# Attention's transposes as 64-row array tiles, its scores in one four-bank tile, and eight blocks per evacuation

## The chip, the cores and the metric

The kernel runs on one core of a Trainium2 chip. The core has TensorE (PE in the rows; PEld is its weight load), VectorE (DVE), ScalarE (ACT), GpSimd (POOL) and SyncE (SP), each with its own queue of instructions that it works off in order; they wait for each other through semaphores. The metric is the device time of one execution in microseconds, as the median of several runs.

## The reference

Attention with a learned relative bias, and behind it two layers of experts. Attention has 2 batches, 8 heads, 576 positions and head size 64; everything is float32.

```python
scores = scale * np.matmul(q, k.transpose(0, 1, 3, 2))
psi_rel = np.log1p(np.abs(rel)); psi_i = np.log1p(np.maximum(pos[:, None], 1.0))
h = np.maximum((psi_rel / psi_i)[..., None] @ w1 + b1, 0.0)      # 32 hidden units
scores = scores + (h @ w2).transpose(2, 0, 1)[None, :, :, :]
attn = np.exp(scores - np.max(scores, axis=-1, keepdims=True))
attn = attn / (np.sum(attn, axis=-1, keepdims=True) + 1e-09)
x = np.matmul(attn, v)                        # then as 1152 rows of 512
out = sum(p[:, e:e+1] * (np.maximum(x @ w1[e], 0) @ w2[e]) for e in range(4))
# second layer: 8 experts, gates by 8 rounds of row and column normalisation
```

## The kernel before

Attention is cut into 36 units, numbered k = 0 to 35: 128 rows of the scores of one pair of heads (p) of one batch (b), by row tile t; in units 8 to 11 (t = 4) the 64 left-over rows of both batches share a unit. One loop over k writes the instructions of four units in different steps, and each engine executes them in the order written. With `u` for the unit a step belongs to, loop step k does this:

- `emit_x(k - 4)`: VectorE multiplies the finished output by one over the sums.
- `emit_S(k)`: TensorE makes the scores (12 matmuls; head 0 on array rows 0 to 63, head 1 on rows 64 to 127) into two PSUM tiles `sc`, one for each head, of two banks each. Behind them in the same tile come two transposes of unit k - 2, its "tail": the last 128 columns of the probabilities (64 per head), and `spread`, one over the sums copied out to 128 columns. Once the bias groups are done the tail goes to a tile `tl` and is written by `emit_T`.
- `emit_max(k)`: VectorE adds the bias and takes the row minimum of the negated scores, one instruction per head (L399).
- `emit_recip2(k - 1)`: VectorE's reciprocal, then GpSimd's copy to `spread`.
- `emit_exp(k, 0)` and `emit_exp(k, 1)`: ScalarE's exponentials, one per head (L412).
- `emit_T(k - 2)`: eight transposes of 128 x 128 (L444) into `tp0` and `tp1`, one bank each; `emit_evac` copies them to SBUF (`at`): four blocks (0), the tail (2), and after the second exponential the other four (1), by ScalarE while there are bias groups and by VectorE after that.
- `groups(1)`: one bias group, while there are any (`made < NGR`): TensorE's `bps` (L331), two ScalarE copies to `bsts` that empty it (L360), a store to DRAM. `bps` is one buffer. `hids` on VectorE makes the next group's operands.
- `emit_P(k - 3)`: probabilities times values (`po`, L470).

Bias groups last until k = 24. Beside attention the loop prepares the experts: `pieces` splits the input for layer 1 into two parts (L103 and L104; k = 16 to 18 and from 23), and from k = 28 the first expert weights are split, a high part by ScalarE (L169) and a low part by GpSimd (L170). At k = 36 the experts' first products start between the last steps of attention, and the tiles of the products take over the banks of the scores.

Of the kernel before, what the change touches and what calls it, by code (L numbers as in the profile page):

```python
# [9 lines left out]
F32 = mybir.dt.float32  # L10
# [38 lines left out]
def attn_moe_moe(ctx: ExitStack, tc: tile.TileContext, pack, keep, rel, qT, kT, vT, w, out):  # L49
# [134 lines left out]
    def attention(moe):  # L184
# [137 lines left out]
        def emit_bias_mm(g):  # L322
            _, _, n, nb = ranges(g)
            if nb == 1 and (made >= FIRST or made % 3 == 1):
                o = pt.tile([128, 1, 512], F32, tag="bps", name=f"bps{g}", bufs=1)
            else:
                o = ps.tile([128, 2, 512], F32, tag="sc", name=f"bps{g}", bufs=2)
# [42 lines left out]

        def emit_S(u):
            t, p, b = units[u]
            o = [ps.tile([128, 2, 512], F32, tag="sc", name=f"sc{u}{h}", bufs=2) for h in range(2)]

            todo = [(b, 0, 128, x, y) for x, y in ((0, 1), (1, 0), (0, 0))] if t < 4 else [(0, 0, 64, None, None), (1, 64, 64, None, None)]
            for j in range(2):
                for i, (bb, c, n, x, y) in enumerate(todo):
                    for h in range(2):
                        d = slice(64 * h, 64 * h + 64)
                        a, m = (qq[t, p][:, x], kk[p, bb][:, y]) if t < 4 else (rawq[t, p], rawk[p, bb])  # L380
                        pe.matmul(  # L381
                            out=o[h][c:c + n, j, 0:288],
                            lhsT=a[d, 128 * bb + c:128 * bb + c + n],
                            rhs=m[d, 288 * j:288 * j + 288],
                            start=t == 4 or i == 0,
                            stop=t == 4 or i == len(todo) - 1,
                        )
            for h in range(2):
                scps[u, h] = o[h]
            if 2 <= u and made < NGR:  # L390
                emit_tail(u - 2, sm[u - 2], o[1][:, :, 288:416])

        def emit_max(u):
            t, p, b = units[u]
# [31 lines left out]
            )  # L426

        tps = {}

        def emit_tail(u, s, o):  # L430

            pe.transpose(o[:, 1, :], s[:, 512:640], ident)  # L432
            pe.transpose(o[:, 0, :], spread.pop(u), ident)
            tps[u, 2] = o

        def emit_T(u):
            s = sm.pop(u)
            if (u, 2) not in tps:
                o = pt.tile([128, 1, 512], F32, tag="bps", name=f"tl{u}", bufs=1)
                emit_tail(u, s, o[:, 0, 0:256].rearrange("p (a c) -> p a c", a=2))  # L440
            for h in range(2):
                o = pt.tile([128, 4, 128], F32, tag=f"tp{h}", name=f"tp{u}{h}", bufs=1)
                for j in range(4):
                    pe.transpose(o[:, j, :], s[:, 640 * h + 128 * j:640 * h + 128 * j + 128], ident)  # L444
                tps[u, h] = o
        def emit_evac(u, h, eng):
            o = tps.pop((u, h))
            shape = [128, 4 if h < 2 else 2, 128]
            a = atb.tile(shape, F32, tag=f"at{h}", name=f"at{u}{h}", bufs=2)
# [4 lines left out]
            at_t[u, h] = a  # L454

        def emit_P(u):
            t, p, b = units[u]
            if b == 0:
                po[t, p] = po_all[:, tps_.index((t, p)) % 2, :]
            o = po[t, p]  # L460
            a = [at_t.pop((u, h)) for h in range(3)]
            rc[u] = a[2][:, 0, :]
            for bb in [b] if t < 4 else [0, 1]:
                n = 128 if t < 4 else 64
                c0, i0 = (128 * bb, 0) if t < 4 else (64 * bb, 64 * bb)
                for j in range(5):
                    for h in range(2):
                        col = (2 * bb + h) * D
                        rhs = a[h][:, j, i0:i0 + n] if j < 4 else a[2][:, 1, i0:i0 + n]
# [40 lines left out]
        order = list(range(8)) + list(range(32, NGR)) + list(range(8, 32))  # L510
        made = 0
        started = 0

        def hids(k, engs=()):
            nonlocal started
# [49 lines left out]
        ti, work, first_split = 0, [], None  # L565
        for k in range(U + 3):
            first = False
            if k < U:
                t, p, b = units[k]
                first = b == 0  # L570
# [15 lines left out]
            elif k == U:  # L586
# [453 lines left out]
```

## Time and profile before

| | us |
|---|---|
| median of 3 runs | 1346.22 (1346.18 to 1347.33) |
| profiled execution, whole | 1347.24 |
| its span in the profile | 1345.5 |
| TensorE busy, whole span | 1332.1 (99%) |
| VectorE, ScalarE, GpSimd busy | 780.0, 518.8, 433.3 |
| scores of unit 4 start | 47.66 |
| scores of unit 25 start (first unit without a bias group) | 138.93 |
| first expert product starts | 177.38 |

The profile is one execution. Busy time of TensorE is modelled, since its matmuls overlap; distances between starts say more. The chain of waits follows the work that ended last back from the end: where it stays on one engine, that engine was never kept waiting there.

### The profile page before, as it was taken

To read this page: it belongs to the slowest core of one execution; us is meant where nothing else is said; L and a number is where in the kernel's file an instruction comes from. 1 tells how busy PE (TensorE), PEld (TensorE's weight loads), DVE (VectorE), ACT (ScalarE), POOL (GpSimd) and SP (SyncE) were. 2 spreads that over 40 slices of the span, in tenths; PEclk is the share of its full clock that TensorE was granted. 3 is DMA by queue.
4 is the path that set the end of the run, shared out by engine and by line. 5 is a ranking of instruction groups with operands and counts; after the bars stand their busy time and mean duration, and the time that the engine had idled before them with its cause. 6 is when DMAs were issued, how large, how long until landed. Compare 5 with 4: busy or idle time off the path is not lost.

```text
span 1345.5 us, 22481 instructions
## 1 busy us (share of the span) xinstructions
PE 1332.1 (99%) x8783; PEld 1163.9 (87%) x8783; DVE 780.0 (58%) x1771; ACT 518.8 (39%) x1230; POOL 433.3 (32%) x455
## 2 busy tenths in 40 slices
PE   7999999999999999999999999999999999999998
PEld 4776888898898898898888988998988988988987
DVE  8788977463563553765764554644635635645533
ACT  6888863341331422443342421422422413313311
POOL 4533433260440530361440530621612603504400
PEclk9999999999999999999999999999999999999999
DMA  7875411130120110020120110210210201201010
GB/s 230 229 200 144 145 64 63 32 95 1 37 90 1 63 64 1 32 71 25 58 68 1 63 63 1 85 41 1 94 32 32 92 4 32 95 0 63 32 40 32
DMA packets 34313, 84.67 MB, mean 63 GB/s; under 512 B 8864, under 2 KB 9120, under 8 KB 34208
## 3 DMA queue, kind: packets, MB, share of 16 engines
q1 hardware_dynamic: 31184, 75.60, 18.0%
q0 software_dynamic: 2880, 7.34, 2.0%
q8 instruction: 69, 1.13, 0.3%
q10 hardware_dynamic: 144, 0.29, 0.1%
q14 instruction: 36, 0.29, 0.1%
HBM read 69.97 MB, written 13.25 MB: 62 GB/s over the span
## 4 chain that ended last, share of the span: by engine, by line
PE 94%; DVE 3%; ACT 1%; DMA 1%; issue 0%; SPq 0%; DVEq 0%; ACTq 0%
PE y L779 44%; PE B L700 17%; PE A L700 11%; PE C L700 11%; PE po L470 3%; PE sc L381 2%; PE tp L444 2%; PE bps L331 1%; ACT bsts L360 1%; DVE rows L801 0%; PE sc L432 0%; PE turn L868 0%; DVE wt L166 0%; DMA bt<-bd 0%; DVE hids L317 0%
## 5 line engine op out<-in xcount | busy, mean ns | idle before, releaser
L779 PE MATMUL y<-gb,h 128*128 128x512 f32 x2592 | 714.2, 396 | 0.0
L779 PEld LDWEIGHTS y<-gb,h 128*128 128x128 f32 x2592 | 451.0, 188 | 55.6
L170 POOL TENSOR_TENSOR gb<-rawb,gb 128x512 fp32r<-128x512 f32 x94 | 122.7, 1322 | 626.6 <-ACT gb L169 620.0
L708 DVE TENSOR_TENSOR u<-B,s 128x320 f32<-128x320 f32 (+1 forms) x192 | 87.9, 458 | 335.7 <-PE B L700 335.7
L711 ACT ACTIVATE h<-c 128x320 fp32r<-128x320 f32 (+1 forms) x288 | 119.8, 439 | 369.4 <-DVE c L708 367.9
L714 DVE SCALAR_TENSOR_TENSOR h<-c,h 128x320 fp32r<-128x320 f32 (+1 forms) x288 | 177.2, 632 | 51.0 <-ACT h L711 46.1
L170 POOL TENSOR_TENSOR ga<-rawa,ga 128x512 fp32r<-128x512 f32 x94 | 128.1, 1382 | 3.2 <-ACT ga L169 3.2
L170 POOL TENSOR_TENSOR ga<-wt,ga 128x512 fp32r<-128x512 f32 x94 | 106.6, 1153 | 25.4 <-ACT ga L169 12.4
L708 DVE TENSOR_TENSOR c<-C,u 128x320 f32<-128x320 f32 (+1 forms) x192 | 87.2, 454 | 38.4 <-PE C L700 34.6
L722 ACT ACTIVATE s<-A 128x320 f32<-128x320 f32 (+1 forms) x96 | 39.4, 411 | 166.5 <-PE A L700 166.3
L169 ACT ACTIVATE gb<-rawb 128x512 fp32r<-128x512 f32 x96 | 60.0, 626 | 85.2 <-DMA rawb<-in_w 85.2
L711 ACT ACTIVATE h<-A 128x320 fp32r<-128x320 f32 (+1 forms) x96 | 38.9, 405 | 136.5 <-PE A L700 136.3
L708 DVE TENSOR_TENSOR c<-B,s 128x320 f32<-128x320 f32 (+1 forms) x96 | 43.9, 457 | 76.3 <-PE B L700 75.3
L700 PE MATMUL C<-x20S,ga 128*128 128x320 f32 x384 | 66.7, 309 | 0.0
L700 PE MATMUL B<-x20S,ga 128*128 128x320 f32 x384 | 66.6, 309 | 0.0
L700 PE MATMUL A<-x20A,ga 128*128 128x320 f32 x384 | 66.6, 309 | 0.0
L700 PEld LDWEIGHTS A<-x20A,ga 128*128 128x128 f32 x384 | 61.5, 188 | 5.7
L700 PEld LDWEIGHTS C<-x20S,ga 128*128 128x128 f32 x384 | 61.3, 188 | 5.6
L700 PEld LDWEIGHTS B<-x20S,ga 128*128 128x128 f32 x384 | 61.3, 188 | 5.6
L412 ACT ACTIVATE s<-s,stat 128x576 f32<-128x576 f32 x72 | 55.7, 774 | 19.8 <-DVE stat L399 19.5
L700 PEld LDWEIGHTS C<-x21S,ga 128*128 128x128 f32 x384 | 54.4, 188 | 6.3 <-DVE c L708 0.7
L700 PEld LDWEIGHTS A<-x21A,ga 128*128 128x128 f32 x384 | 54.6, 189 | 5.6
(183 smaller groups left out, 1913.8 us busy)
## 6 DMA issues: line engine op xcount, KB each, us to landing
rawa<-in_w SPq DMA_DIRECT2D x48, 512.0 KB, 4.0
rawb<-in_w SPq DMA_DIRECT2D x48, 512.0 KB, 4.9
bd<-bsts SPq DMA_DIRECT2D x36, 295.5 KB, 3.7
bt<-bd SPq DMA_DIRECT2D x13, 512.0 KB, 4.8
qr<-in_qT POOLq DMA_DIRECT2D x40, 64.0 KB, 3.2
kr<-in_kT POOLq DMA_DIRECT2D x16, 144.0 KB, 3.5
V<-in_vT POOLq DMA_DIRECT2D x4, 512.0 KB, 7.4
out<-rows SPq DMA_DIRECT2D x8, 256.0 KB, 2.1
```

Source lines behind the costliest of these rows:

```text
L169: sc.activation(out=z(0), in_=src, func=AF.Copy)
L170: lo.tensor_tensor(out=z(1), in0=src, in1=z(0).bitcast(F32), op=ALU.subtract)
L381: pe.matmul(out=o[h][c:c + n, j, 0:288], lhsT=a[d, 128 * bb + c:128 * bb + c + n], rhs=m[d, 288 * j:288 * j + 288], start=t == 4 or i == 0 ...
L412: sc.activation(out=s, in_=s, func=AF.Exp, scale=-1.0, bias=stat[u][:, h:h + 1], accum_out=stat[u][:, 2 + h:3 + h],)
L444: pe.transpose(o[:, j, :], s[:, 640 * h + 128 * j:640 * h + 128 * j + 128], ident)
L470: pe.matmul(out=o[64 * h:64 * h + 64, c0:c0 + n], lhsT=V[p][:, j, col:col + D], rhs=rhs, start=j == 0, stop=j == 4,)
L700: pe.matmul(out=ban[o], lhsT=a, rhs=x[:, z, k, :], start=not more and i == 0, stop=i == 5, skip_group_check=more,)
L708: ve.tensor_tensor(out=t[o], in0=ban[a], in1=t[b], op=ALU.add)
L711: sc.activation(out=h[f][:, 0, half, :], in_=src, func=AF.Relu)
L714: ve.scalar_tensor_tensor(out=h[f][:, 1, half, :], in0=src, scalar=0.0, in1=h[f][:, 0, half, :].bitcast(F32), op0=ALU.max, op1=ALU.subtract,)
L722: sc.activation(out=t["s1"], in_=ban["A"], func=AF.Copy)
L779: pe.matmul(out=self.y[t], lhsT=a, rhs=x, start=g == 0 and f == 0 and i == 0, stop=g == NP - 1 and f == 1 and i == 2,)
```

## The change

From unit 4 on (`FOUR = 4`) both heads' scores lie in one PSUM tile of four banks, with one buffer. The tail of unit k - 2 is transposed into it ahead of the scores. Transposes work on 64 array rows: one of 128 x 128 becomes two, with rows 0 to 63 and 64 to 127 of the probabilities as operands and 64 moving columns, each into a bank of its own. The sixteen results lie in one tile of two banks, and one ScalarE instruction copies all eight blocks out (`emit_evac(.., 3, ..)`). The tail's copy is now the first thing that ScalarE does in a loop step. In the units after the bias groups VectorE no longer copies four of the blocks. The last two units keep whole transposes and two copies. From unit 2 on, the order of ScalarE's copies is already the new one, with whole transposes at first.

```diff
         def emit_S(u):
             t, p, b = units[u]
-            o = [ps.tile([128, 2, 512], F32, tag="sc", name=f"sc{u}{h}", bufs=2) for h in range(2)]
+            if u >= FOUR:
+                x = ps.tile([128, 4, 512], F32, tag="sc", name=f"sc{u}", bufs=1).rearrange("p (h j) c -> p h j c", h=2)
+                o = [x[:, h] for h in range(2)]
+                emit_tail(u - 2, sm[u - 2], x[:, :, 0, 288:416])
+            else:
+                o = [ps.tile([128, 2, 512], F32, tag="sc", name=f"sc{u}{h}", bufs=2) for h in range(2)]
...
-            if 2 <= u and made < NGR:
-                emit_tail(u - 2, sm[u - 2], o[1][:, :, 288:416])
+            if 2 <= u < FOUR:
+                emit_tail_whole(u - 2, sm[u - 2], o[1][:, :, 288:416])
...
+        halves = [slice(64 * r, 64 * r + 64) for r in range(2)]
 
         def emit_tail(u, s, o):
-
+            for w, x in ((1, s[:, 512:640]), (0, spread.pop(u))):
+                for r, d in enumerate(halves):
+                    pe.transpose(o[:, r, 64 * w:64 * w + 64], x[d], ident[d, d])
...
         def emit_T(u):
             s = sm.pop(u)
-            if (u, 2) not in tps:
-                o = pt.tile([128, 1, 512], F32, tag="bps", name=f"tl{u}", bufs=1)
-                emit_tail(u, s, o[:, 0, 0:256].rearrange("p (a c) -> p a c", a=2))
-            for h in range(2):
-                o = pt.tile([128, 4, 128], F32, tag=f"tp{h}", name=f"tp{u}{h}", bufs=1)
-                for j in range(4):
-                    pe.transpose(o[:, j, :], s[:, 640 * h + 128 * j:640 * h + 128 * j + 128], ident)
-                tps[u, h] = o
+            at_t[u, 0] = a = atb.tile([128, 8, 128], F32, tag="at", name=f"at{u}", bufs=2)
+            cols = [s[:, 640 * h + 128 * j:640 * h + 128 * j + 128] for h in range(2) for j in range(4)]
+            if FOUR <= u + 2 < U:
+                o = pt.tile([128, 2, 8, 64], F32, tag="tp", name=f"tp{u}", bufs=1)
+                for i, x in enumerate(cols):
+                    for r, d in enumerate(halves):
+                        pe.transpose(o[:, r, i, :], x[d], ident[d, d])
+                to = a.rearrange("p i (r c) -> p r i c", r=2)
...
+            if k == FOUR:
+                st_sc.close()
+                ps, four = pool("ps4", PSUM, stack=st_sc, side="left"), True
...
             if k < U:
+                if k >= 2:
+                    emit_evac(k - 2, 2, sc)
                 emit_exp(k, 0)
             if k >= 2 and k - 2 < U:
                 emit_T(k - 2)
-                emit_evac(k - 2, 0, sc)
-                emit_evac(k - 2, 2, sc)
+                one = k < U
+                emit_evac(k - 2, 3 if one else 0, sc)
+                if k >= U:
+                    emit_evac(k - 2, 2, sc)
             if k < U:
                 emit_exp(k, 1)
             groups(1)
             if k >= 2 and k - 2 < U:
-                emit_evac(k - 2, 1, sc if made < NGR else ve)
+                if not one:
+                    emit_evac(k - 2, 1, ve)
```

ScalarE's queue in unit 20 stood so before. Names carry the unit, then the head or copy (`at182` is copy 2, the tail, of unit 18), and a buffer number; in brackets is whose counter the instruction waits for. The first exponential's wait for VectorE is for the first head's minimum, the tail's is for the second's.

```order
L412 ACTIVATE s20_1815,stat20_1814<-s20_1815,stat20_1814 128x576 [waits DVE_49,Pool_49]
L453 ACTIVATE at180_1832<-tp180_1822 128x512 [waits PE_49]
L453 ACTIVATE at182_1834<-sc201_1799 128x256 [waits DVE_49]
L412 ACTIVATE s20_1815,stat20_1814<-s20_1815,stat20_1814 128x576
L360 ACTIVATE bsts_113<-bps27_1837,cst_97 128x144 [waits DMAHW0_49,PE_49]
L360 ACTIVATE bsts_113<-bps27_1837,cst_97 128x448 [waits Activation_49]
L453 ACTIVATE at181_1845<-tp181_1827 128x512
```

The same place in the changed kernel:

```order
L478 ACTIVATE at182_1897<-sc20_1892 128x2x2x64 [waits DVE_49,PE_49]
L417 ACTIVATE s20_1911,stat20_1910<-s20_1911,stat20_1910 128x576 [waits Pool_49]
L478 ACTIVATE at18_1919<-tp18_1920 128x2x8x64 [waits PE_49]
L417 ACTIVATE s20_1911,stat20_1910<-s20_1911,stat20_1910 128x576
L360 ACTIVATE bsts_113<-bps27_1939,cst_97 128x144 [waits DMAHW0_49,PE_49]
L360 ACTIVATE bsts_113<-bps27_1939,cst_97 128x448 [waits Activation_49]
```

The tail's copy moved from third place to first. Its wait for VectorE is for both minima (they signal once, after the second), the first exponential has no wait for VectorE of its own any more, and the two copies of four blocks are one of eight.

TensorE's queue in unit 20 before, from the last score matmuls on:

```order
L381 MATMUL sc200_1798<-kk00_191,qq20_1570 128x288
L381 MATMUL sc201_1799<-kk00_191,qq20_1570 128x288
L432 MATMUL sc201_1799<-kept_73,s18_1675 128x128
L433 MATMUL sc201_1799<-kept_73,spread18_1754 128x128 [waits Pool_49]
L444 MATMUL tp180_1822<-kept_73,s18_1675 128x128 [waits PE_49]
L444 MATMUL tp180_1822<-kept_73,s18_1675 128x128 x3
L444 MATMUL tp181_1827<-kept_73,s18_1675 128x128 [waits PE_49,Activation_49]
L444 MATMUL tp181_1827<-kept_73,s18_1675 128x128 x3
L331 MATMUL bps27_1837<-hids_112,w2n_98 32x448 [waits PE_49]
```

The same unit in the changed kernel:

```order
L441 MATMUL sc20_1892<-kept_73,s18_1759 128x64 [waits Activation_49]
L441 MATMUL sc20_1892<-kept_73,s18_1759 128x64
L441 MATMUL sc20_1892<-kept_73,spread18_1844 128x64 [waits Pool_49]
L441 MATMUL sc20_1892<-kept_73,spread18_1844 128x64
L386 MATMUL sc20_1892<-kk00_191,qq20_1646 128x288 x12
L459 MATMUL tp18_1920<-kept_73,s18_1759 128x64 [waits Activation_49]
L459 MATMUL tp18_1920<-kept_73,s18_1759 128x64 x15
L331 MATMUL bps27_1939<-hids_112,w2n_98 32x448 [waits PE_49,Activation_49]
```

The tail's transposes, with the wait for GpSimd's `spread`, moved from behind the scores to ahead of them. The first of them waits for ScalarE's copy of the tail before, which frees the one tile of scores; the bias product's wait for ScalarE is for the second copy of the group before.

## Rows read from the trace of the kernel before

**Rows 1.** Windows: length, busy PE, PEld, DVE, ACT, POOL, clock, DMA share, GB/s.

```profile
47.66:138.93 91.27, 90.96 (x1150) 65.17 (x1148) 74.72 (x243) 81.65 (x203) 32.40 (x75) 1.00 0.68 186
138.93:177.38 38.45, 38.39 (x464) 32.75 (x462) 35.87 (x117) 33.70 (x97) 19.19 (x40) 1.00 0.44 133
```

**Rows 2.** Chain of waits (start us, us, what), bias products of 304 and 432 columns.

```profile
79.95 0.65 PE bps L331 x8
...
112.51 0.99 PE sc L381 x10
...
114.74 0.86 PE bps L331 x8
...
116.84 0.99 PE sc L381 x12
```

**Rows 3.** Timeline of units 19 and 20: start us, us, instruction, idle before.

```profile
113.43 0.14 PEld L432 LDWEIGHTS sc<-kept,s 128*128 128x128 f32 x1 [0.16 <-issue]
...
113.70 1.04 PE L444 MATMUL tp<-kept,s 128*128 128x128 f32 x8
113.78 0.75 DVE L399 CUSTOM_DVE_ANT_0 s<-sc,rows 128x576 f32<-128x576 f32 x1
...
114.46 0.09 DVE L399 DVE_READ_ACCUMULATOR2_ANT stat<- 128x1 f32 x1
114.46 0.76 DVE L399 CUSTOM_DVE_ANT_0 s<-sc,rows 128x576 f32<-128x576 f32 x1
114.64 0.78 ACT L412 ACTIVATE s<-s,stat 128x576 f32<-128x576 f32 x1 [0.43 <-DVE stat L399]
...
114.67 0.93 PE L331 MATMUL bps<-hids,w2n 128*32 128x432 f32 x8
...
115.41 0.58 ACT L453 ACTIVATE at<-tp 128x512 f32<-128x512 f32 x1
...
115.53 1.31 PE L470 MATMUL po<-at,V 128*64 128x128 f32 x20
...
115.89 0.37 ACT L453 ACTIVATE at<-sc 128x256 f32<-128x256 f32 x1
116.15 0.77 ACT L412 ACTIVATE s<-s,stat 128x576 f32<-128x576 f32 x1
...
116.78 1.06 PE L381 MATMUL sc<-kk,qq 64*128 64x288 f32 x12
...
116.91 1.04 ACT L360 ACTIVATE bsts<-bps,cst 128x160 f32<-128x160 f32 x2
...
117.87 0.76 DVE L399 CUSTOM_DVE_ANT_0 s<-sc,bt 128x576 f32<-128x576 f32 x1 [0.49 <-PE sc L381]
```

**Rows 4.** Timeline, unit 32 into unit 33: weight split, spread and scores.

```profile
165.09 0.50 ACT L103 ACTIVATE x10S<-rows 128x128 fp32r<-128x128 f32 x2
165.49 0.62 ACT L169 ACTIVATE ga<-rawa 128x512 fp32r<-128x512 f32 x1
166.19 1.28 POOL L170 TENSOR_TENSOR ga<-rawa,ga 128x512 fp32r<-128x512 f32 x1 [0.15 <-ACT ga L169]
...
166.97 1.06 PE L381 MATMUL sc<-kk,qq 64*128 64x288 f32 x12
167.41 0.36 POOL L424 COPY spread<-stat 128x128 f32<-128x128 f32 x1
...
168.13 0.27 PE L433 MATMUL tl<-kept,spread 128*128 128x128 f32 x1
```

**Rows 5.** Timeline of TensorE: scores of units 29 and 35.

```profile
152.80 1.05 PE L381 MATMUL sc<-kk,qq 64*128 64x288 f32 x12
...
173.92 1.05 PE L381 MATMUL sc<-kk,qq 64*128 64x288 f32 x12
```

**Rows 6.** Timeline of ScalarE at the hand-over to the experts.

```profile
177.40 0.77 ACT L412 ACTIVATE s<-s,stat 128x576 f32<-128x576 f32 x1
...
178.56 0.44 ACT L722 ACTIVATE s<-A 128x320 f32<-128x320 f32 x1 [0.30 <-PE A L700]
```

More of the change, by code (lines that the diff above doesn't have):

```diff
@@ L326, in emit_bias_mm @@
             else:
-                o = ps.tile([128, 2, 512], F32, tag="sc", name=f"bps{g}", bufs=2)
+                o = ps.tile([128, 4 if four else 2, 512], F32, tag="sc", name=f"bps{g}", bufs=1 if four else 2)[:, 0:2, :]
             n //= nb
@@ L428, in attention @@
         tps = {}
+        FOUR = 4
+        halves = [slice(64 * r, 64 * r + 64) for r in range(2)]
         def emit_tail(u, s, o):
+            for w, x in ((1, s[:, 512:640]), (0, spread.pop(u))):
+                for r, d in enumerate(halves):
+                    pe.transpose(o[:, r, 64 * w:64 * w + 64], x[d], ident[d, d])
+            at_t[u, 1] = atb.tile([128, 2, 128], F32, tag="at2", name=f"at{u}2", bufs=2)
+            tps[u, 2] = o.rearrange("p r (w c) -> p r w c", w=2), at_t[u, 1].rearrange("p w (r c) -> p r w c", r=2)
@@ L432, in emit_tail, with emit_tail_whole @@
+        def emit_tail_whole(u, s, o):
+            at_t[u, 1] = atb.tile([128, 2, 128], F32, tag="at2", name=f"at{u}2", bufs=2)
             pe.transpose(o[:, 1, :], s[:, 512:640], ident)
             pe.transpose(o[:, 0, :], spread.pop(u), ident)
-            tps[u, 2] = o
+            tps[u, 2] = o, at_t[u, 1]
         def emit_T(u):
             s = sm.pop(u)
-            if (u, 2) not in tps:
-                o = pt.tile([128, 1, 512], F32, tag="bps", name=f"tl{u}", bufs=1)
-                emit_tail(u, s, o[:, 0, 0:256].rearrange("p (a c) -> p a c", a=2))
@@ L441, in emit_T @@
-            for h in range(2):
-                o = pt.tile([128, 4, 128], F32, tag=f"tp{h}", name=f"tp{u}{h}", bufs=1)
-                for j in range(4):
-                    pe.transpose(o[:, j, :], s[:, 640 * h + 128 * j:640 * h + 128 * j + 128], ident)
-                tps[u, h] = o
+            at_t[u, 0] = a = atb.tile([128, 8, 128], F32, tag="at", name=f"at{u}", bufs=2)
[6 more added lines that the diff above has]
+                to = a.rearrange("p i (r c) -> p r i c", r=2)
+            else:
+                if u + 2 >= U:
+                    o = pt.tile([128, 1, 512], F32, tag="bps", name=f"tl{u}", bufs=1)
+                    emit_tail_whole(u, s, o[:, 0, 0:256].rearrange("p (a c) -> p a c", a=2))
+                o = pt.tile([128, 2, 4, 128], F32, tag="tp", name=f"tp{u}", bufs=1)
+                for i, x in enumerate(cols):
+                    pe.transpose(o[:, i // 4, i % 4, :], x, ident)
+                to = a.rearrange("p (h j) c -> p h j c", h=2)
@@ L446, in emit_evac @@
+            for r in range(2):
+                tps[u, r] = o[:, r], to[:, r]
+            tps[u, 3] = o, to
         def emit_evac(u, h, eng):
-            o = tps.pop((u, h))
-            shape = [128, 4 if h < 2 else 2, 128]
-            a = atb.tile(shape, F32, tag=f"at{h}", name=f"at{u}{h}", bufs=2)
+            o, a = tps.pop((u, h))
             if eng is ve:
@@ L453, in emit_evac @@
                 sc.activation(out=a, in_=o, func=AF.Copy)
-            at_t[u, h] = a
         def emit_P(u):
@@ L460, in emit_P @@
             o = po[t, p]
-            a = [at_t.pop((u, h)) for h in range(3)]
-            rc[u] = a[2][:, 0, :]
+            a, a2 = at_t.pop((u, 0)), at_t.pop((u, 1))
+            rc[u] = a2[:, 0, :]
             for bb in [b] if t < 4 else [0, 1]:
@@ L468, in emit_P @@
                         col = (2 * bb + h) * D
-                        rhs = a[h][:, j, i0:i0 + n] if j < 4 else a[2][:, 1, i0:i0 + n]
+                        rhs = a[:, 4 * h + j, i0:i0 + n] if j < 4 else a2[:, 1, i0:i0 + n]
                         pe.matmul(
@@ L512, in attention @@
         started = 0
+        four = False
         def hids(k, engs=()):
```

## The prediction

> **What bounds the kernel now.** I read the page first, then windows by stage, then the chain of waits, then the timeline of one unit. TensorE is busy nearly throughout, so the question is whether it is merely full or also the thing waited for. The change touches attention from unit 4 on. The scores of unit 4 start at 47.66 and the experts' first product at 177.38; two stages lie between. TensorE is busy 90.96 of 91.27 us in the first and 38.39 of 38.45 in the second, and ScalarE has little room either, 81.65 and 33.70 [rows 1]. The first stage, units 4 to 24, has a bias group (`bps`) in each unit. Its chain runs on TensorE alone: from scores to scores 112.51 to 116.84, 4.33 us, of which 0.86 is the bias product [rows 2]. The second stage has no bias groups and is paced at 3.47 us a unit (138.93 to 152.80 for four units) [rows 1, 5].
>
> So work taken from TensorE is a gain up to the next limit. I look for that limit in what the order puts on ScalarE.
>
> **The change, part by part.** All figures in us.
>
> *Transposes.* Eight full-array transposes take 1.04 from first start to last end, about 0.11 each [rows 3]. They become sixteen of half the moving columns, on two row halves. If the halves run side by side, a pair takes half of 0.11, the eight pairs 0.44. No transposes on half the array are in the trace; the nearest rows are the scores, which do run on 64 rows: twelve in 1.06, at most 0.09 each [rows 3], which for sixteen gives 1.4. I take 0.45, since the scores stream 288 columns and these 64. The four half transposes of the tail then cost 0.1 to 0.36; I take 0.15. The tail now has the scores' form of the array, so one change of form goes, in which TensorE idles 0.16 before the tail [rows 3]. On TensorE alone a unit with a bias group would fall from 4.33 to 0.15 + 0.82 (scores, 0.99 in the chain less that step) + 0.55 (transposes and the step to the bias product) + 0.86 + 1.25 = 3.63.
>
> *Evacuation.* A copy of 512 columns keeps ScalarE 0.48 (115.41 to 115.89), one of 256 keeps it 0.26 (115.89 to 116.15) [rows 3]: 0.22 per 256, so 1024 keep it 0.48 + 0.43 = 0.90 and end about 1.0 after they start. In the first stage this replaces two ScalarE copies of 0.48 and saves 0.06. In the second it replaces one, the other having been VectorE's; ScalarE gains 0.43 a unit. The window says that ScalarE has 4.75 free over eleven units there [rows 1], 0.43 each.
>
> *Scores in one tile, and the copy of the tail first.* This decides. Before, ScalarE starts a unit with the first exponential, which waits for the first min-reduction only; the tail's copy follows behind a copy of four blocks. Now the tail's copy is at the head of ScalarE's unit, and since it reads the tile that both reductions read, it waits for the second. Everything behind it on ScalarE waits too: both exponentials, the copy of eight blocks, and the two copies that free the single bias buffer. The next bias product on TensorE waits for these, and behind it stand the values' products and the next scores. That closes a loop over two units:
>
> bias product to values 0.86 (114.67 to 115.53); values to scores 1.25 (115.53 to 116.78); tail transposes 0.15; scores to first reduction 1.09 (116.78 to 117.87); both reductions 1.44 (113.78 to 115.22), 0.09 to ScalarE (114.55 to 114.64); tail's copy 0.26, exponential 0.77, eight blocks 0.90, exponential 0.76, bias copies 1.04 (116.91 to 117.95); 0.05 back to TensorE. Sum 8.66, 4.33 a unit [rows 3]. In the kernel before the same loop takes 0.86 + 1.25 + 1.09 + 0.68 (first reduction only) + 0.18 + 0.77 + 0.48 + 0.26 + 0.76 + 1.04 + 0.05 = 7.42, 3.7 a unit, which is why TensorE hid it.
>
> So TensorE's saving of 0.7 turns into a wait in front of the bias product. Of that product's length only half counts in the loop. It takes 0.86 with 432 columns and 0.65 with 304 [rows 2], so 0.79 at 389, the mean of the 21 units. At 0.65 the unit goes from 4.12 to 4.22, at the mean from 4.26 to 4.295. Over 21 units: **+0.7**. With the tail at 0.36 it is +2.9; with the tail at 0.1 and 0.1 less in the other hops, -1.
>
> The Trainium skill has a rule that speaks against this exchange: "TensorEngine Tiling (Array Packing)", Performance Considerations, says that tiling speeds TensorE but not the emptying of PSUM, and to use ScalarE and VectorE both for it. The trace agrees on the place, since ScalarE's free 0.43 a unit is just what the second stage's extra copy takes. By the rule alone the second stage's first term would be 0 and not a gain, and the sum half a microsecond higher; the terms below don't use it.
>
> *Second stage, units 25 to 35.* Without bias groups the loop runs through the transposes, which wait for the copy of eight blocks: transposes to values 0.53, 1.25, 0.15, 1.09, 1.53, 0.26 + 0.77, copy 1.0, 0.05: 6.63 over two units, 3.3 (3.8 at the slow bound of the transposes). Four units at 3.35 instead of 3.47: **-0.5**.
>
> From unit 28 on ScalarE and GpSimd also split the first expert weights, and the tail's order matters again. GpSimd copies `spread` behind its half of the split: ScalarE's half starts at 165.49, GpSimd's at 166.19 for 1.28, `spread` at 167.41, done at 167.77 [rows 4]. Now it is needed at 168.13, after the scores of 166.97. In the new order the tail's transposes stand ahead of the scores, so scores due at 166.97 would wait until 167.8. The loop over two units: 2.28 from ScalarE's half to `spread`, 0.07, two transposes 0.1, 1.09, 1.53, ScalarE's 0.26 + 0.77 + 0.90 + 0.76, 0.4 for the two splits of the layer's input (165.09 to 165.49), back at the next weight split: 8.16, 4.08 a unit. Now these units take 3.52 (152.80 to 173.92 for six) [rows 5]. Unit 29 comes in on the shorter loop and pays the first wait whole, 4.8 against 3.5: **+1.3**; units 30 to 34: 5 x (4.08 - 3.53) = **+2.7**; unit 35, with no split left behind it, 3.1 against 3.5: **-0.4**.
>
> *Hand-over.* Now the last exponential starts with the first product (177.40), and ScalarE's copy of that product at 178.56 lets the third start [rows 6]. In the new order tail's copy, first exponential and eight blocks come first, so the copy's end moves from 1.6 after the first product's start to 2.8 (2.4 for the end of the last exponential, 0.44 for the copy). The third product, which could start at about 1.9 with two products through, waits for it: **+0.9**. Behind that all is shifted and nothing else changed.
>
> Sum +0.7 - 0.5 + 1.3 + 2.7 - 0.4 + 0.9 = +4.7. The profiled execution took 1347.24 (span 1345.5, 1.7 around it), 1.0 above the median of 1346.22; 1351.9 against it, and against the median **1350.9**.
>
> **Rivals.**
>
> *A, TensorE's saving arrives.* If the two-unit loop were under 8.0, a unit of the first stage would go below 4.0, and at 3.56, TensorE's own sum at the mean, the stage would give 21 x 0.7 = 15: 1346.2 - 15 + 4 = 1335; half of it 1343. For it: TensorE is the only engine without idle time now [rows 1]. Against it: the hops are rows, and only the tail's 0.15 is a guess. It decides at 8.52, twice 4.26, and my sum at the mean is 8.59; so a small gain here is near, a large one far. The Trainium skill, in the same "TensorEngine Tiling (Array Packing)", Theoretical Speedup, states up to twofold for a contraction of 64 rows; by it alone TensorE gets its saving, and this rival is the result.
>
> *B, a draw.* The first stage at 8.3 a loop gives 3 back and the second takes 4: 1346.2 to 1347.5.
>
> *C, the halves don't overlap.* Sixteen transposes at 0.11 take 1.75, the tail 0.44: TensorE's unit is 0.44 + 0.82 + 1.85 + 0.79 + 1.25 = 5.15 in the first stage, +0.9 x 21, and the second's first loop grows by 1.6 over two units, +0.7 x 11: 1373. Against it: twelve scores on row halves in 1.06, where one alone streams more than twice the columns of a transpose.
>
> **How the numbers follow.** Chances: forecast 0.60, A 0.17, B 0.15, C 0.08. About 0.2%, 2.7 us, is what a measurement of this kernel can tell from no change. The forecast's own range is 1347.5 to 1356, from the tail's bounds and the slow transposes. Slower takes C and most of the forecast, 0.62; the same takes B and the forecast's lower end, 0.21; faster is A, 0.17. The range 1342 to 1357 leaves out C and the larger half of A.
>
> **What would show it.** Right: in units 4 to 24 TensorE idles before the bias product, released by ScalarE's bias copies, for 0.4 to 0.8 a unit; ScalarE's longest wait is the tail's copy for the second reduction; scores start every 4.2 to 4.4; from unit 29 the tail's `spread` transposes wait for GpSimd, and scores come every 4.1; the granted clock stays at 1.00. Wrong: score starts under 4.0 apart in the first stage (A), half transposes more than 0.09 apart (C), or no wait for GpSimd in units 30 to 35.

## The result, and the profile after

The changed kernel takes 1355.7 us in the median (1354.1 to 1357.1) against 1346.2: a ratio of 1.0069, 95% interval 1.0052 to 1.0087, so 9.5 us slower. Forecast were 1350.9, slower, in a range of 1342 to 1357. The profiled execution took 1357.07, its span 1355.0 against 1345.5. The four timings lie two by two, 1354.1 and 1354.5 at a mean granted clock of 1.000, 1356.9 and 1357.1 at 0.997; with the clock alike the change costs 8.2 (see *Sum* below).

The windows of the changed kernel for the two stages, scores of unit 4 to those of unit 25 and from there to the experts' first product, answer to [rows 1]; the other two rows lie ahead of the change. Columns are those of [rows 1].

```profile
49.37:142.82 93.45, 80.58 (x1358) 57.96 (x1360) 74.71 (x242) 79.66 (x180) 31.84 (x74) 1.00 0.67 182
142.82:185.53 42.71, 34.66 (x573) 29.07 (x571) 31.81 (x106) 37.79 (x98) 18.27 (x39) 1.00 0.40 120
33.00:36.00 3.00, 2.21 (x13) 1.94 (x14) 2.13 (x5) 1.31 (x2) 2.94 (x6) 0.50 0.69 200
36.00:41.00 5.00, 5.00 (x33) 3.25 (x33) 3.15 (x10) 2.50 (x6) 3.56 (x7) 0.62 0.90 253
```

TensorE has lost its grip on both stages: it is busy 80.58 of 93.45 where it was busy 90.96 of 91.27, and 34.66 of 42.71. The work did shrink by 10 us in the first stage, and the stage still grew by 2.2.

What it waits for, in the waits of units 8 to 24 (total us, times, longest):

```profile
PEld bps L331 <- ACT bsts L360: 11.5, 15, 1.1
PE bps L331 <- ACT bsts L360: 9.2, 13, 1.0
ACT at L478 <- DVE stat L427: 7.9, 12, 2.3
```

and in those of the second stage:

```profile
PEld sc L441 <- POOL spread L429: 5.4, 7, 1.4
...
PE sc L441 <- POOL spread L429: 4.3, 5, 1.2
PEld sc L441 <- ACT at L478: 4.0, 10, 0.6
```

The bias product waits for ScalarE's copies of the bias before, ScalarE's copy of the tail for VectorE (L427 is the reciprocal, which follows the second reduction directly), the tail's transposes for GpSimd: the three waits of the forecast. In the changed kernel the half transposes are L459, ScalarE's copies L478, the tail's transposes L441, the scores L386. Its timeline, cut at five places (units 6, 19, 28, 30 and the hand-over), answers to [rows 3, 4, 6]:

```profile
55.15 1.22 POOL L245 DMA_DIRECT2D qr<-in_qT  x2
...
56.36 0.80 POOL L205 DMA_DIRECT2D V<-in_vT  x1
...
57.12 1.29 POOL L208 DMA_DIRECT2D V<-in_vT  x2
...
58.41 0.30 POOL L429 COPY spread<-stat 128x128 f32<-128x128 f32 x1
...
58.77 0.28 PE L441 MATMUL sc<-kept,spread 64*128 64x64 f32 x2 [0.68 <-POOL spread L429]
...
112.56 0.66 PE L459 MATMUL tp<-kept,s 64*128 64x64 f32 x16
...
114.18 0.91 PE L331 MATMUL bps<-hids,w2n 128*32 128x416 f32 x8 [0.96 <-ACT bsts L360]
...
115.02 1.31 PE L494 MATMUL po<-at,V 128*64 128x128 f32 x20
...
115.44 1.02 ACT L478 ACTIVATE at<-tp 128x1024 f32<-128x1024 f32 x1
...
116.26 0.28 PE L441 MATMUL sc<-kept,s 64*128 64x64 f32 x2
...
116.35 0.78 ACT L417 ACTIVATE s<-s,stat 128x576 f32<-128x576 f32 x1
...
116.40 1.04 PE L386 MATMUL sc<-kk,qq 64*128 64x288 f32 x12
...
152.29 1.23 POOL L245 DMA_DIRECT2D qr<-in_qT  x2 [0.26 <-issue]
...
153.51 0.30 POOL L429 COPY spread<-stat 128x128 f32<-128x128 f32 x1
...
153.87 0.28 PE L441 MATMUL sc<-kept,spread 64*128 64x64 f32 x2 [0.66 <-POOL spread L429]
...
160.40 1.33 POOL L170 TENSOR_TENSOR gb<-rawb,gb 128x512 fp32r<-128x512 f32 x1
...
161.67 0.35 POOL L429 COPY spread<-stat 128x128 f32<-128x128 f32 x1
...
162.08 0.27 PE L441 MATMUL sc<-kept,spread 64*128 64x64 f32 x2 [1.16 <-POOL spread L429]
...
187.79 0.43 ACT L755 ACTIVATE s<-A 128x320 f32<-128x320 f32 x1
...
188.27 1.14 PE L733 MATMUL A<-x10A,ga 128*128 128x320 f32 x6 [0.72 <-ACT s L755]
```

Sixteen half transposes take 0.66 where sixteen of 0.11 would take 1.75, so the halves do run side by side; the tail costs TensorE 0.14 (116.26 to 116.40), and a copy of eight blocks keeps ScalarE 0.91 (115.44 to 116.35). In unit 30 `spread` stands behind the weight split and the scores wait 1.16 for it, as forecast. In units 6 and 28 it stands behind something else: GpSimd issues loads, of q for 1.2 and of V for 2.1 more, and the tail's transposes wait 0.68 and 0.66.

The span's 9.5 divide by score starts so: ahead of unit 4, 1.7; first stage 2.2 (91.27 to 93.45); second stage 4.3 (38.45 to 42.71); from the first to the third expert product 0.9 (1.86 to 2.74); the rest 0.5, which was not taken apart (they add up to 9.6 by rounding).

### The profile page after: what moved, and what is told of

The parts are those of the page before. It is cut to its first block, busy times and chain, and to the rows that moved or that the text cites. A ratio compares the mean times of both kernels' runs of the same rounds, so it can differ in the third digit from the quotient of the medians.

```text
span 1355.0 us, 23068 instructions
## 1 busy us (share of the span) xinstructions
PE 1319.6 (97%) x9103; PEld 1153.3 (85%) x9103; DVE 779.0 (57%) x1759; ACT 522.1 (39%) x1208; POOL 433.0 (32%) x455
## 3 DMA queue, kind: packets, MB, share of 16 engines
q8 instruction: 71, 1.16, 0.4%
## 4 chain that ended last, share of the span: by engine, by line
PE 86%; DVE 5%; ACT 5%; issue 2%; POOL 1%; DMA 1%; SPq 0%; ACTq 0%; POOLq 0%; DVEq 0%
PE y L812 43%; PE B L733 17%; PE C L733 11%; PE A L733 11%; ACT s L417 2%; DVE s L404 1%; ACT at L478 1%; PE sc L386 1%; ACT bsts L360 1%; PE bps L331 1%; PE po L494 1%; DVE rows L834 0%; DVE wt L166 0%; PE turn L901 0%; DMA rawb<-in_w 0%
## 5 line engine op out<-in xcount | busy, mean ns | idle before, releaser
L733 PE MATMUL C<-x20S,ga 128*128 128x320 f32 x384 | 66.7, 309 | 0.0
L733 PEld LDWEIGHTS B<-x21S,ga 128*128 128x128 f32 x384 | 54.2, 188 | 5.7 <-issue 0.2
```

The costliest lines, as they stand in the source:

```text
L733: pe.matmul(out=ban[o], lhsT=a, rhs=x[:, z, k, :], start=not more and i == 0, stop=i == 5, skip_group_check=more,)
```

## The experiments

The table puts all runs side by side: start of unit 4's scores, length of the two stages and of the hand-over (first to third expert product) in each run's profile, and the median of its timings. A loop, below, is the distance between the scores of every second unit, from 4 to 6, 6 to 8 and so on.

| run | unit 4 | first | second | hand-over | median |
|---|---|---|---|---|---|
| before | 47.66 | 91.27 | 38.45 | 1.86 | 1346.2 |
| changed | 49.37 | 93.45 | 42.71 | 2.74 | 1355.7 |
| tail_behind | 45.95 | 91.75 | 40.41 | 2.72 | 1350.5 |
| spread_on_vector | 46.05 | 92.48 | 43.01 | 2.67 | 1353.4 |
| copy_second | 46.71 | 87.45 | 40.50 | 2.00 | 1345.6 |
| halves_alone | 47.59 | 91.65 | 37.48 | 1.86 | 1346.9 |
| second_and_behind | 45.62 | 84.98 | 39.72 | 1.99 | 1343.2 |
| second_whole | 49.48 | 90.08 | 41.02 | 1.92 | 1350.8 |
| split_copy | 47.14 | 87.07 | 48.65 | 1.86 | 1351.8 |
| blocks_last | 47.20 | 91.36 | 39.36 | 2.00 | 1348.6 |
| changed_again | 49.69 | 93.93 | 42.72 | 2.75 | 1354.6 |
| before_copy_first | 46.21 | 96.97 | 38.48 | 1.86 | 1352.1 |
| tail_apart | 45.90 | 86.52 | 39.72 | 2.23 | 1342.7 |
| v_loads_elsewhere | 46.22 | 91.69 | 42.69 | 2.75 | 1351.8 |

The stages are those of one execution each. second_and_behind, split_copy and tail_apart have the same instructions up to unit 25, and their first stages are 84.98, 87.07 and 86.52; so a difference of 2 us between two first stages shows nothing by itself. Where unit 4 starts goes with the clock (last section).

**tail_behind.** The tail's place alone undone (`four_banks` is the tile `x`).

```diff
-                emit_tail(u - 2, sm[u - 2], x[:, :, 0, 288:416])
+                four_banks = x
 ...
-            if 2 <= u < FOUR:
+            if u >= FOUR:
+                emit_tail(u - 2, sm[u - 2], four_banks[:, :, 0, 288:416])
+            elif u >= 2:
```

> The changed kernel, but with the four half transposes of the tail written behind the scores in the same four-bank tile instead of ahead of them; ScalarE's order stays as changed. Theory 1 (spread's place costs): the scores no longer wait for GpSimd's copy to spread, so the two long loops of units 4 to 8 (9.5 us each against 8.7) come down by about 0.8 each, and the second stage (units 25 to 35 to the experts' first product, 42.7) by about 3, while the loops of units 8 to 24 stay at 8.6 to 8.8: about 1351. Theory 2 (ScalarE's order alone sets the pace, GpSimd only looks late): no change, 1355 to 1356. Theory 3 (the one tile of four banks is the cost, since scores wait for both reductions and for the copy of the tail): no change either, and the scores' longest wait is for the copy of the tail.

1350.5, ratio to before 1.0028 (1.0018 to 1.0038). Units 4 to 8 take 17.46 instead of 19.02, the second stage 2.3 less, and units 8 to 24 the same 69.5: theory 1, with less in the second stage than the 3 expected.

**spread_on_vector.**

```diff
-            gp.tensor_copy(
+            ve.tensor_copy(
                 spread[u].rearrange("p (h d) -> p h d", h=2), ...
```

> The changed kernel, but spread is made by VectorE right behind its reciprocal instead of by GpSimd; TensorE's and ScalarE's orders are untouched. Theory 1 (GpSimd's queue: the issue of the loads of V and q in units 4 to 8, the weight split from unit 28): the waits before the tail's transposes of spread go, 0.8 in each of the first two loops and about 3 in the second stage: about 1351. Theory 2 (ScalarE's order sets the pace): 1355 to 1356, with the same loops of 8.6 to 8.8 and a second stage still over 42. The copy costs VectorE some 0.2 a unit, which has 13 of 74 us free from unit 8 to 24.

1353.4 (ratio 1.0045, 1.0031 to 1.0058). Units 4 to 8 take 17.35 instead of 19.02, as theory 1 has it; the second stage gains nothing, and there theory 1 misses. Its timeline shows what else waits (units 30 and 31):

```profile
157.10 1.33 POOL L170 TENSOR_TENSOR gb<-rawb,gb 128x512 fp32r<-128x512 f32 x1
...
157.22 1.37 DVE L104 TENSOR_TENSOR x10S<-rows,x10S 128x128 fp32r<-128x128 f32 x1
...
161.78 0.38 ACT L478 ACTIVATE at<-sc 128x256 f32<-128x256 f32 x1 [1.46 <-DVE stat L427]
...
162.22 0.28 PE L441 MATMUL sc<-kept,s 64*128 64x64 f32 x2 [0.54 <-ACT at L478]
...
162.78 0.28 DVE L104 TENSOR_TENSOR x10S<-t,x10S 128x128 fp32r<-128x128 f32 x1
```

Once `spread` is early, ScalarE's copy of the tail waits 1.46 for the second reduction, the scores for that copy. VectorE lost 1.09 ahead of that: a subtraction of 0.28 took 1.37 beside GpSimd's weight split of 1.33, and ended 0.16 behind it. The Trainium skill, "SBUF — State Buffer" (SBUF: two separate sides), has VectorE's operations with two SBUF inputs and GpSimd's take turns at one pair of ports for a whole instruction; the two rows agree. So in the second stage two waits lie over one another, and taking one away shows the other.

**copy_second.**

```diff
             if k < U:
+                emit_exp(k, 0)
                 if k >= 2:
                     emit_evac(k - 2, 2, sc)
-                emit_exp(k, 0)
```

> The changed kernel, but ScalarE does the first exponential ahead of the copy of the tail, so that the wait for the second reduction stands behind that exponential; the copy of eight blocks stays behind both. Theory 1 (the loop over two units through the bias product, which in the changed kernel holds the tail's copy and with it the second reduction): the loop loses the second reduction, some 0.75, less 0.1 of hop, so 8.0 instead of 8.7 over two units; units 8 to 24 give 16 x 0.33 = 5 us, the two long loops little and the second stage at most 1: about 1350. Theory 2 (the one tile of four banks): the scores now get their tile 0.8 later, when the tail's copy is done, and nothing is gained: 1354 to 1358. Theory 3 (TensorE's own work, the half transposes being dearer than they look): no change, and TensorE has no wait before the bias product.

1345.6 (ratio 0.9987, 0.9978 to 0.9996): nine less than the changed kernel, by one line moved (10.1 and 9.0 less than its two medians, 1355.7 and 1354.6; the two stages and the hand-over together are 9.0 shorter). The loops of units 8 to 24 are 8.04 to 8.26 but for one of 8.74 (8.0 expected), the first stage falls by 6.0, the second by 2.2. Units 8 to 24 give 4.0 of the 5 expected; units 4 to 8 (1.3), the second stage and the hand-over (0.7) give more than theory 1 had, whose sum was about 1350. So the second reduction, in the loop by way of the tail's copy, is the largest single cost of the change. In its waits of units 8 to 24 the bias product still waits for ScalarE, but 4.1 instead of 9.2:

```profile
PEld bps L331 <- ACT bsts L360: 6.3, 13, 1.1
...
PE bps L331 <- ACT bsts L360: 4.1, 9, 0.9
```

**halves_alone.** The kernel before with half transposes only.

```diff
-            for h in range(2):
-                o = pt.tile([128, 4, 128], F32, tag=f"tp{h}", ...)
-                for j in range(4):
-                    pe.transpose(o[:, j, :], s[:, 640 * h + 128 * j:...], ident)
+            o = [pt.tile([128, 8, 64], F32, tag=f"tp{r}", ...) for r in range(2)]
+            for i in range(8):
+                for r in range(2):
...
+                    pe.transpose(o[r][:, i, :], s[d, c:c + 128], ident[d, d])
```

> The kernel before, with one part of the change alone: each of the eight big transposes as two on 64 array rows, in all units, each row half into a bank of its own, copied out by the same two instructions of 512 columns in the same places of the queues as before. Tail, scores, their tiles and ScalarE's order are those of the kernel before. Theory 1 (the half transposes run side by side and save TensorE about 0.45 a unit; ScalarE's and GpSimd's places ate it): in units 4 to 24 the loop of 7.4 over two units is no bound, TensorE is, and a unit falls by 0.3 to 0.45: 21 x 0.4 = 8 us, in the second stage up to 2: 1336 to 1340. Theory 2 (the save is only in how the records look, or ScalarE's 4 us of work a unit in the first stage is a bound of its own): 1344 to 1347.

1346.9 (ratio 0.9997, 0.9988 to 1.0006): no gain in sum (the second stage is 1.0 shorter), and theory 1 falls. Its timeline, units 15 and 16:

```profile
96.05 0.14 PEld L432 LDWEIGHTS sc<-kept,s 128*128 128x128 f32 x1 [0.17 <-issue]
...
96.42 0.63 PEld L446 LDWEIGHTS tp<-kept,s 64*128 64x128 f32 x16 [0.17 <-PE sc L432]
...
97.12 0.83 PE L331 MATMUL bps<-hids,w2n 128*32 128x368 f32 x8
...
100.24 0.59 ACT L459 ACTIVATE at<-tp 128x512 f32<-128x512 f32 x1
...
100.88 0.57 PEld L446 LDWEIGHTS tp<-kept,s 64*128 64x128 f32 x15 [0.27 <-ACT at L459]
```

Two things eat the saving. The tail between the scores and the half transposes stands on the full array, so the form now changes twice, 0.17 each, where it was once 0.16 before. And a loop is in the way that the forecast had not seen: the last copy of four blocks, behind the bias copies, frees the bank for the next transposes (the 0.27 of the last row). From its end: 0.05 to the transposes, 0.64 to the bias product (100.88 to 101.52), 0.78 to the values, 1.24 to the scores, 1.09 to the first reduction, 0.86 to the first exponential, then ScalarE's row: 0.77, 0.48, 0.26, 0.77, 0.94 and 0.59. Sum 8.47 over two units; measured were 8.45 to 8.51 from unit 12 to 18.

**second_and_behind.** The edits of copy_second and tail_behind together.

> The changed kernel with both edits: ScalarE does the first exponential ahead of the copy of the tail (as in the run copy_second, 1345.6), and the tail's transposes stand behind the scores (as in tail_behind, 1350.5). Theory 1 (two separate terms: the second reduction in the loop of the bias product, 0.3 a unit, and GpSimd's late spread, 0.8 in each of two loops of the first stage and some in the second): they add. From copy_second the two long loops of units 4 to 8 fall from 8.8 and 8.9 to 8.1, and the second stage from 40.5 to about 39: 1342 to 1343. Theory 2 (both hide the same wait, that for the tail's copy which frees the one tile of scores): no more than copy_second alone, 1345 to 1346.

1343.2 (ratio 0.9972, 0.9962 to 0.9983), faster than both kernels. Units 4 to 8 take 16.07, 1.6 less than in copy_second; there the two edits add. Units 8 to 24 take 64.69, but 66.2 and 66.7 in the profiles of tail_apart and split_copy, against 65.55 in copy_second: no gain is shown there, and none was expected. The second stage takes 39.72, 3.0 less than the changed kernel's, where the edits gave 2.2 and 2.3 by themselves; there they add only in part. The profiled execution took 1340.8, 2.4 less than the median.

**second_whole.**

```diff
-                o = pt.tile([128, 2, 8, 64], F32, tag="tp", name=f"tp{u}", bufs=1)
+                o = pt.tile([128, 2, 4, 128], F32, tag="tp", name=f"tp{u}", bufs=1)
                 for i, x in enumerate(cols):
-                    for r, d in enumerate(halves):
-                        pe.transpose(o[:, r, i, :], x[d], ident[d, d])
+                    pe.transpose(o[:, i // 4, i % 4, :], x, ident)
...
```

> The kernel of copy_second, but with the eight big transposes whole (128 x 128 on the full array) in all units, in the same two-bank tile and with the same one copy of 1024; the tail stays as 64-row halves. It tells what the halves give where ScalarE's order lets it arrive. Theory 1 (a half transpose pair costs 0.05 against 0.11, and two changes of the array's form of about 0.16 are saved): TensorE's unit grows by 0.39 + up to 0.32 and bounds the first stage again at 4.3 or more: 8.05 becomes 8.6 to 8.9 over two units, 1352 to 1356. Theory 2 (ScalarE's loop alone decides and TensorE's saving is worth nothing even here): 1345 to 1347.

1350.8 (ratio 1.0029, 1.0018 to 1.0041). From unit 4 to the first product it takes 131.1 against copy_second's 128.0: with ScalarE's order mended the half transposes are worth some 3 us there, less than theory 1 had them; loops of 8.3 to 8.7 from unit 8 on instead of 8.6 to 8.9. Some of the 5 between the medians lies ahead of unit 4 (49.48 against 46.71), which is no part of the edit; its two executions at a mean clock of 0.999, as copy_second has it, took 1349.0 and 1349.2, 3.5 more.

**split_copy.** From second_and_behind: `one = k < U and made < NGR`, so that VectorE copies one row half in the second stage.

> The kernel of second_and_behind, but in the units without a bias group the eight blocks leave PSUM in two copies again, one row half by ScalarE before the second exponential, the other by VectorE behind it. Theory 1 (in the second stage ScalarE is the later engine, with 37.8 of 42.7 us busy in the changed kernel): the second stage falls by up to 0.4 a unit, to 37 or 38 against about 39 without the edit, so 1 to 2 us. Theory 2 (VectorE, whose reductions the scores' tile waits for, is the later one there): nothing, or up to 1 slower.

1351.8, 8.6 slower than without, more than either theory gave. Its timeline, units 30 and 31, and two windows of it:

```profile
154.64 0.59 ACT L480 ACTIVATE at<-tp 128x512 f32<-128x512 f32 x1
...
155.26 0.69 DVE L478 COPY at<-tp 128x512 f32<-128x512 f32 x1 [1.02 <-ACT at L480]
...
158.87 0.77 ACT L419 ACTIVATE s<-s,stat 128x576 f32<-128x576 f32 x1 [1.97 <-DVE stat L406]
...
165.18 0.77 ACT L419 ACTIVATE s<-s,stat 128x576 f32<-128x576 f32 x1 [3.02 <-DVE stat L406]
...
155.00:160.00 5.00, 3.00 (x52) 2.49 (x50) 4.18 (x14) 2.82 (x10) 0.65 (x2) 1.00 0.45 121
160.00:169.00 9.00, 7.43 (x76) 6.89 (x78) 6.85 (x18) 5.45 (x16) 3.62 (x7) 0.50 0.23 64
```

VectorE's copy is ordered behind ScalarE's and stands there for 1.02, with VectorE's other work and the next reductions behind it; ScalarE then waits 1.97 and 3.02 for them. Why it is ordered so stays open: in halves_alone the two copies write halves of one tile `at` too, and there VectorE's starts ahead of ScalarE's (151.85 and 152.06, unit 28). Part of the time is the clock's: behind 5 us in which TensorE was busy 3.00, it was granted 0.50, or 1.2 GHz, from 160 to 169, so that 48.65 is not the order's alone. An execution with a mean clock of 0.999 still took 1350.9, 7.7 more than the median of second_and_behind; most of the 8.6 is thus the order's. The Trainium skill's advice in "TensorEngine Tiling (Array Packing)", PSUM Bottleneck, to use both engines for the emptying, does not hold in this order of the queues; in halves_alone, where VectorE copies too, the second stage is the shortest of all, 37.48.

**blocks_last.** From second_and_behind: in units with a bias group `emit_evac(k - 2, 3, sc)` stands behind `groups(1)`.

> The kernel of second_and_behind, but in units with a bias group the copy of eight blocks stands behind the two bias copies on ScalarE instead of ahead of the second exponential. Theory 1 (the loop of the bias product over two units, 8.05 in copy_second, holds this copy of 1.02): the loop falls to 7.0 and is no bound any more; ScalarE's own sum of 3.85 a unit is the next: units 8 to 24 take 62 to 63 instead of 65.5, so about 2.5 us less than second_and_behind. Theory 2 (a new loop takes over: copy, half transposes, bias product, bias copies, copy, 1.0 + 0.6 + 0.8 + 1.05 and hops, 3.7 to 4.0 a unit): no gain, and the half transposes wait for the copy in each unit.

1348.6 (ratio 1.0016, 1.0007 to 1.0025): theory 2 has the right wait, though in a loop of two units and not of one. The waits of units 8 to 24:

```profile
PEld tp L461 <- ACT at L480: 9.5, 12, 1.0
...
PE tp L461 <- ACT at L480: 7.7, 10, 0.9
```

It is the loop of halves_alone again, with the copy of 1.01 at its end: 0.05 + 0.65 + 0.8 + 1.24 + 1.09 + 0.86 + 0.77 + 0.26 + 0.77 + 0.94 + 1.01 = 8.44, measured 8.5 to 8.8.

**changed_again.** The changed kernel once more.

> The changed kernel itself once more, for more timings and a second profile. In the first profile the scores of unit 2 start 1.3 later than in the profile of before, and 2.8 to 3.3 later than in those of copy_second, tail_behind and second_and_behind, in a stretch (33 to 41 us) where TensorE's granted clock is 0.5 to 0.6 in some executions and 1.00 in others, of all kernels alike. Theory 1 (that is chance of an execution and no part of the change): the timings lie in two clumps some 2.5 apart, as the timings of before do, the median comes out at 1354 to 1356, and from the scores of unit 4 to the experts' first product it takes 136 us as in the first profile (136.2). Theory 2 (the changed kernel falls into the low clock there always): all timings within 1356.5 and 1357.5.

1354.6 (ratio 1.0057, 1.0045 to 1.0070). Its timings were 1357.4 and four between 1354.4 and 1354.7; the profiled one is the 1357.4, with a clock of 0.60 from 33 to 36 us, and from unit 4 to the first product it takes 136.7: theory 1. Unit 2 starts at 40.1 again in this slower execution; its 1.3 of the first profile goes with the clock and is no cost of the change.

**before_copy_first.** The kernel before with the tail's copy ahead of the first exponential, where the tail stands in the scores' tile.

```diff
+            early = (k - 2, 2) in tps
+            if early:
+                emit_evac(k - 2, 2, sc)
             if k < U:
                 emit_exp(k, 0)
...
```

> The kernel before, with one part of the change alone: in units with a bias group ScalarE copies the tail ahead of the first exponential, so that it waits for the second reduction first. Transposes, tiles, and the place of the tail's transposes are those of before. Theory 1 (TensorE's own work hides the loop): the loop over two units grows from 7.42 by the second reduction, to about 8.1, still under TensorE's 8.5, so 1346 to 1348 and score starts as before. Theory 2 (the order costs by itself): the bias product waits for ScalarE in most units, and the first stage grows by 3 or more: 1350 and over.

1352.1 (ratio 1.0041, 1.0029 to 1.0054), the first stage 5.7 longer: theory 1 falls, and with it the forecast's picture of the kernel before. Its timeline, unit 16:

```profile
101.64 0.76 DVE L399 CUSTOM_DVE_ANT_0 s<-sc,bt 128x576 f32<-128x576 f32 x1 [0.61 <-PE sc L381]
...
101.95 0.59 ACT L453 ACTIVATE at<-tp 128x512 f32<-128x512 f32 x1
...
102.59 0.66 PE L444 MATMUL tp<-kept,s 128*128 128x128 f32 x4 [0.18 <-ACT at L453]
...
103.12 0.38 ACT L453 ACTIVATE at<-sc 128x256 f32<-128x256 f32 x1 [0.58 <-DVE stat L399]
...
103.18 0.85 PE L331 MATMUL bps<-hids,w2n 128*32 128x384 f32 x8
```

The last copy of four blocks (101.95) lets the second half of the transposes start (102.59). The same loop as in halves_alone, with 1.48 from the first reduction to the tail's copy (101.64 to 103.12) where 0.86 led to the exponential, and 0.59 of transposes: 0.05 + 0.59 + 0.78 + 1.24 + 1.09 + 1.48 + 0.28 + 0.76 + 0.48 + 0.75 + 0.95 + 0.59 = 9.04. Measured: 8.99 to 9.14 up to unit 18.

**tail_apart.** From second_and_behind: in the second stage the tail goes whole to the bias bank, as in the kernel before.

> The kernel of second_and_behind, but in the units without a bias group the tail is transposed whole into the free bias bank, as in the kernel before, behind the scores and ahead of the half transposes, and copied out behind the eight blocks. Theory 1 (in the second stage the scores wait for the copy of the tail, which frees the one tile of scores: 6.1 us in ten waits): the waits go, and the second stage falls from 39.7 to 37 to 38: 1341 to 1342. Theory 2 (ScalarE's sum of work there, 3.4 to 3.6 a unit with the weight split, is the bound and the waits are only its shadow): second stage 39 or over, 1343.

1342.7 (ratio 0.9969, 0.9958 to 0.9981), and the second stage 39.72 as without: theory 2, the waits for the tail's copy were a shadow. ScalarE has little room there, in second_and_behind by its window of that stage 38.26 of 39.72:

```profile
130.60:170.32 39.72, 32.27 (x574) 28.73 (x573) 34.50 (x106) 38.26 (x100) 18.71 (x40) 1.00 0.44 130
```

**v_loads_elsewhere.** In `load_v`, `sy.dma_start` for `gp.dma_start`.

> The changed kernel, but the loads of V in steps 0, 2, 4 and 6 are issued by SyncE instead of GpSimd; nothing else. Theory 1 (in units 4 to 8 GpSimd comes late to spread because it issues three V loads, 2.1 us in a row, and two q loads ahead of it): the two loops of 9.5 fall to 8.7, the first stage by 1.6, the second stage stays at 42.7: 1353.5 to 1354.5. Theory 2 (GpSimd is late there for another reason, its wait for the second exponential's sums): no change, 1355 to 1356.

1351.8 (ratio 1.0035, 1.0022 to 1.0049). Units 4 to 8 take 17.26 instead of 19.02, the second stage stays: theory 1. The median fell by 2.8 from that of changed_again, 1.0 more than the stage; what the loads' new place does ahead of unit 4 was not taken apart.

## Why the direction was right and the size too small

*Transposes and copies.* The tail's 0.15 and the copy's 0.90 and 1.0 measured 0.14, 0.91 and 1.02. The half transposes were sized too cheap: 0.55 with the step to the bias product, measured 0.64 and 0.70 (100.88 to 101.52 and 96.42 to 97.12 in halves_alone). TensorE was to save 0.7 a unit; by its busy time it saved 0.5 (90.96 and 80.58 over 21 units, 4.33 and 3.84). It did not matter, since TensorE sets nothing there any more.

*First stage, +0.7.* The loop of 8.66 was right: units 8 to 24 measured 8.6 to 8.8, and from unit 8 to 25 the stage grew by 0.1, where the term has 0.6 for these 17 units. It set out from 4.26 a unit, TensorE's sum in one unit at the mean width, while [rows 1] have 91.27 over 21 units, 4.35. copy_second took the named piece, the second reduction, out of it and got the loop expected. Mis-sized were units 4 to 8, +2.05: the forecast knew that the tail now waits for `spread` ahead of the scores, but priced GpSimd's queue only where it splits weights. In units 6 and 8 it issues q and V loads ahead of `spread`; tail_behind and v_loads_elsewhere each gave 1.6 to 1.8 of it back, the second by moving the V loads alone.

*The kernel before.* "7.42 over two units, which is why TensorE hid it" was wrong: it counted the loop by the bias bank and missed the one by the last copy of four blocks, 8.4 to 8.5 by the hops of halves_alone, level with TensorE's own 8.5. Its wait shows in the kernel before behind the scores of unit 18:

```profile
109.77 0.66 PE L444 MATMUL tp<-kept,s 128*128 128x128 f32 x4 [0.31 <-ACT at L453]
```

That is why the half transposes alone gain nothing, and why the copy's order alone makes the first stage 5.7 longer. It left the sum unharmed, because the changed kernel has no such last copy.

*Second stage, -0.5 + 1.3 + 2.7 - 0.4.* Measured by score starts: units 25 to 28 +0.5, unit 29 +1.5, units 30 to 34 +2.6 (4.06 each, 4.08 forecast), unit 35 -0.4. Only the first is off, by 1.0, and it lies at unit 28, whose scores start 4.38 behind those of unit 27 (3.47 before): GpSimd's q loads again. Without the wait for `spread`, in tail_behind and spread_on_vector, that step takes 3.51 and 3.69. From unit 29 on the agreement is partly luck. Scores come 4.8 to 5.0 and 3.3 to 3.7 apart in turn, two units take 8.26, 8.53 and 8.46 and not 8.16, and five units from a short one to a short one happen to average 4.06. And the wait for `spread` is the cost of the whole stage only in part: tail_behind takes 2.3 of 4.3 away, and spread_on_vector showed a second wait of the same size beneath it.

*Hand-over, +0.9.* Measured 0.88; with the exponential first 0.1.

*Sum.* +4.7 becomes 2.2 + 4.3 + 0.9 = 7.3 in the priced parts, the difference being GpSimd's load issues in units 6, 8 and 28, a term that the forecast put at nothing. The 1.7 ahead of unit 4 had no term: 0.4 lie between units 2 and 4, where the copies' order is already changed, and 1.3 ahead of unit 2, where nothing is changed yet and the clock was lower (last section). Without that 1.3, and with the 0.5 behind, the parts make 8.2; so do the executions at a mean clock of 0.999 or more, 1354.6 in the median of six against 1346.4 in that of 14 of the kernel before. That the measured 9.5 is twice the forecast's 4.7 is thus in part the clock's doing.

*Rivals.* A did not come, but one line of ScalarE's order parts it from the result: with that line moved (copy_second) the first stage is 87.45, 3.8 less than before and not 15 less, since a loop of 8.1 still bounds it. B needed a first stage 3 shorter, and it grew by 2.2. C is excluded by 0.66 for sixteen.

What stays open: why the second stage of the best versions is 1.3 longer than before's. ScalarE's extra copy fits, but the one try to hand it to VectorE was spoiled by its place. The one tile of four banks is in every version built on the changed kernel and was not tried by itself; it may have a part in this.

## What to carry to other kernels

Before pricing a saving on a full engine, list every loop through a single buffer, also those that are only just hidden: here one of 8.45 lay under TensorE's 8.5. A wait that moves to the head of an in-order queue costs all that stands behind it, so put first what waits for least. And where an operand is now needed earlier, walk its maker's whole queue, issues of loads included, at each unit, not only where heavy work stands.

## What was not expected of the hardware

Executions of one kernel differ by what TensorE's clock does early in attention, ahead of unit 2. In the changed kernel's profile the granted clock is 0.50 from 33 to 36 us, 1.2 GHz, and 0.62 from there to 41 (0.61 and 0.90 in that of before); in copy_second, with the same instructions up to there, it is 1.00:

```profile
33.00:36.00 3.00, 2.62 (x27) 2.34 (x31) 2.77 (x9) 1.74 (x5) 2.94 (x6) 1.00 0.74 214
```

In both TensorE was busy 1.5 of the 3 us before (30 to 33), with waits for VectorE and ScalarE of over 1 us each. The low clock puts unit 2's scores at 38.3 to 40.1 instead of 36.4 to 37.3 in the profiles, and it would account for the two clumps of timings of the changed kernel, 2.8 apart: the mean clock is 0.997 in the three later ones and 1.000 in the six others, of which none was profiled.
